# Reordering the start of a fused attention and feed-forward kernel, and moving one transposition from TensorE to DMA

**The chip, the cores and the metric.** The kernel runs on one core of one Trainium2 chip. The metric is the device time of one execution in microseconds; the median of several executions is quoted. The kernel before takes 327.13 us (three runs, 326.89 to 327.17).

Short names used below: TensorE is PE in the profile, its weight loads PEld, VectorE DVE, ScalarE ACT, GpSimd POOL, SyncE SP. A name with a q, such as SPq, is that engine's sequencer, which also issues DMAs.

## The reference

A linear attention (ReLU features weighted by cosine and sine of the position, keys and values summed into one matrix per head) is followed by a feed-forward layer gated with GELU.

```python
# q, k, v: (8 batches, 8 heads, 576 tokens, 64)
q_p, k_p = phi(q), phi(k)                  # relu(x)*cos(pos) next to relu(x)*sin(pos): 128 features
kv  = einsum('bhsf,bhsd->bhfd', k_p, v)
z   = k_p.sum(axis=2)
att = einsum('bhsf,bhfd->bhsd', q_p, kv) / (einsum('bhsf,bhf->bhs', q_p, z)[..., None] + 1e-6)
x   = att laid out as (4608 tokens, 512)
out = (gelu(x @ w_gate) * (x @ w_val)) @ w_out      # 512 -> 1536 -> 512
```

## The kernel before

The attention of one batch has five token tiles, four of 128 tokens and one of 64. The feed-forward layer runs in blocks of tokens: block 0 holds the 576 tokens of batch 0, each later block 512. While block n runs, the attention of batch n + 1 is slipped in between its twelve column tiles. Feed-forward matmuls need the tokens transposed (`xT`). In block 0, and for batch 1, TensorE transposes them into PSUM and another engine copies them out; later batches use a DMA transpose issued by SP.

The parts that matter here (cuts marked):

```python
def x_by_pe(b, t, xb, bank, eng, ..., every=1):      # transposition by TensorE
    ...
    for ct in range(c0, c1):
        nc.tensor.transpose(out=view[:, ct, 0:rows], in_=xb2[...], ...)       # line 343
    cp(xT[...], view[...])                                                    # line 346

def turn_x(b, t, xb):                                # transposition by DMA
    if t < NJ: nc.sync.dma_start_transpose(out=xT[:, :, p0:p0 + 128], in_=xb2)
    else:
        nc.sync.dma_start_transpose(out=xr, in_=xb2)                          # line 208
        nc.gpsimd.tensor_copy(xT[:, :, p0:p0 + 64], xr[:, :, 0:128:2])

# block 0: X(t) = x_by_pe of tile t, Y(t) = its numerators (line 170) and normalization
gate(0, 2, *A, 5); X(2, 0, "v")(); ...
value(0, 2, *A, 7)
gate(0, 3, *A, 4)
Y(3, 0)(); value(0, 3, *A, 2); q_by_pe(0, 4, 3, "s")
gv_unit(0, 0, 256, 128, 5, 6); X(3, 0, "s")()
Y(4, 0)()                                  # writes PSUM banks 0 and 1
gv_unit(0, 1, 256, 128, 4, 7)
...
# before block 1
o_part(0, 3, 5, 0, 5);  x_by_pe(1, 2, y[2], 6, "s")
y4 = numer(1, 4, 0)                        # last 64 tokens of batch 1
o_part(0, 3, 5, 5, 10); x_by_pe(1, 3, y[3], 7, "s")
x_by_pe(1, 4, y4, 6, "v", every=2)
o_part(0, 3, 5, 10, 12)
# block 1: after column tile 0, turn_q(2, ...) issues the DMA transposes of batch 2's queries (line 145);
# after tile 4, kv_half(2, ...) (line 154); within tile 5, the numerators of batch 2's first tile
```

Gate products are line 218, value products 229, output products 259 and, for the last tile, 277.

Of the kernel before, what the change touches and what calls it, by code (L numbers as in the profile page):

```python
# [16 lines left out]
def kernel(  # L17
# [10 lines left out]
    nc = tc.nc  # L28
# [4 lines left out]
    C = H * D  # L33
    J = moe_w_gate.shape[1]
    CT = C // 128
    JT = J // 128
    NJ = 4
# [20 lines left out]
    wo_sb = sb.tile([128, JT, C], BF16, name="wo_sb")  # L58
    xT = sb.tile([128, CT, N_TOK], BF16, name="xT")
    qf = sb.tile([128, H, NJ + 1, D], FP32, name="qf")  # L60
    kf = sb.tile([128, H, NJ + 1, D], FP32, name="kf")
# [68 lines left out]
    def scale(f, j, which, eng, h0=0, h1=H):  # L130
        dst, src = f
        col = (cos_c if which == 0 else sin_c)[:, j:j + 1]
        s, d = src[:, h0:h1, j, :], dst[:, j, h0:h1, which * D:(which + 1) * D]
        if eng == "v":
            nc.vector.tensor_scalar(d, s, col, 0.0, op0=ALU.mult, op1=ALU.max)  # L135
        else:
            nc.scalar.activation(d, s, AF.Relu, scale=col)  # L137
# [30 lines left out]
    def numer_mm(b, t, bank, g, rows=128):  # L168
        for h in range(4 * g, 4 * g + 4):
            nc.tensor.matmul(  # L170
                ps[0:rows, bank + g, (h % 4) * (D + 1):(h % 4 + 1) * (D + 1)],
                lhsT=qT[b % 2][:, t, h, 0:rows],
                rhs=kv[b % 2][:, h, 0:D + 1],
                start=True, stop=True,
            )

    def norm(xb, bank, g0, g1, rows=128):

        n = g1 - g0
        nd = ps[0:rows, bank + g0:bank + g1, 0:4 * (D + 1)].rearrange("p g (h e) -> p g h e", e=D + 1)  # L180
        den = rot.tile([128, 2, 4], FP32, name="den")
        nc.vector.tensor_scalar(den[0:rows, 0:n], nd[:, :, :, D], EPS, None, op0=ALU.add)  # L182
        rec = rot.tile([128, 2, 4], FP32, name="rec")
        nc.vector.reciprocal(rec[0:rows, 0:n], den[0:rows, 0:n])
        nc.vector.tensor_tensor(  # L185
            xb[0:rows, g0:g1], nd[:, :, :, 0:D],
            rec[0:rows, 0:n, :, None].to_broadcast([rows, n, 4, D]), op=ALU.mult,
        )

    def new_xb():  # L190
        return rot.tile([128, 2, 4, D], BF16, name="xb", bufs=4)

    def numer(b, t, bank, rows=128):

        numer_mm(b, t, bank, 0, rows)
        numer_mm(b, t, bank, 1, rows)
        xb = new_xb()
        norm(xb, bank, 0, 2, rows)
        return xb
# [14 lines left out]
    def gate(n, jt, c0, w, gb):  # L214

        p0 = starts[n] + c0
        for ct in range(CT):
            nc.tensor.matmul(  # L218
                ps[:, gb, 0:w], lhsT=wg_sb[:, ct, jt * 128:(jt + 1) * 128],
                rhs=xT[:, ct, p0:p0 + w], start=(ct == 0), stop=(ct == CT - 1),  # L220
            )
        gels[n, jt, c0] = gel = rot.tile([128, 512], FP32, name="gel", bufs=4)
        nc.scalar.activation(gel[:, 0:w], ps[:, gb, 0:w], AF.Gelu)  # L223

    def value(n, jt, c0, w, vb):

        p0 = starts[n] + c0
        for ct in range(CT):
            nc.tensor.matmul(  # L229
                ps[:, vb, 0:w], lhsT=wv_sb[:, ct, jt * 128:(jt + 1) * 128],  # L230
                rhs=xT[:, ct, p0:p0 + w], start=(ct == 0), stop=(ct == CT - 1),
            )
        gel = gels.pop((n, jt, c0))
        nc.vector.tensor_mul(hT[n % 2][:, jt, 64 + c0:64 + c0 + w], gel[:, 0:w], ps[:, vb, 0:w])  # L234

    def gv_unit(n, jt, c0, w, gb, vb, mid=()):
        gate(n, jt, c0, w, gb)
        for f in mid:
            f()
        value(n, jt, c0, w, vb)  # L240
# [15 lines left out]
    def o_part(n, m, bank, j0, j1):  # L256
        c0 = 128 * m - starts[n] + 64
        for jt in range(j0, j1):
            nc.tensor.matmul(  # L259
                ps[:, bank, :], lhsT=hT[n % 2][:, jt, c0:c0 + 128], rhs=wo_sb[:, jt, :],  # L260
                start=(jt == 0), stop=(jt == JT - 1),
            )
        if j1 == JT:
            o_store(m, bank)
# [37 lines left out]
    wo_r = moe_w_out.rearrange("(jt p) c -> p jt c", p=128)  # L302
# [5 lines left out]
    def load_q(b, eng=None):  # L308
        load(qf, q, b, even=eng, odd=eng)

    def load_k(b):
        load(kf, k, b)
# [20 lines left out]
        else:  # L333
            cp(qT[b % 2][:, j, h0:h1, 0:64], qb[:, h0:h1, 0:128:2])

    def x_by_pe(b, t, xb, bank, eng, c0=0, c1=CT, every=1):
        p0 = b * S + t * 128
        cp = nc.vector.tensor_copy if eng == "v" else nc.scalar.copy
        xb2 = xb.rearrange("p g h d -> p (g h d)")
        rows = 128 if t < NJ or every == 2 else 64  # L340
        view = ps[:, bank, 0:256].bitcast(BF16).rearrange("p (c t) -> p c t", c=CT)
        for ct in range(c0, c1):
            nc.tensor.transpose(  # L343
                out=view[:, ct, 0:rows], in_=xb2[0:rows, ct * 128:(ct + 1) * 128], identity=ident[0:rows, 0:rows],
            )
        cp(xT[:, c0:c1, p0:p0 + rows // every], view[:, c0:c1, 0:rows:every])  # L346

    def sq(j, which, eng, *h):
        scale(Q, j, which, eng, *h)
# [37 lines left out]
    numer_mm(0, 1, 0, 1)  # L387
    norm(x1, 0, 0, 2)
    x_by_pe(0, 0, x0, 4, "s", 0, 2)
    dummies(2, 5)  # L390
    x_by_pe(0, 0, x0, 4, "s", 2, 4)
    q_by_pe(0, 2, 3, None)

# [4 lines left out]
    A, Bw = (0, 256), (256, 320)  # L398
    xs = {1: x1}

    def X(t, bank, eng):
        return lambda: x_by_pe(0, t, xs[t], bank, eng)

    def Y(t, bank):
        def f():
            xs[t] = numer(0, t, bank, 128 if t < NJ else 64)
        return f
# [14 lines left out]
    gate(0, 2, *A, 5)  # L422
    X(2, 0, "v")()
    sq(4, 1, "s"), sq(4, 0, "v")
    value(0, 2, *A, 7)
    gate(0, 3, *A, 4)
    Y(3, 0)()
    value(0, 3, *A, 2)
    q_by_pe(0, 4, 3, "s")
    gv_unit(0, 0, 256, 128, 5, 6)  # L430
    X(3, 0, "s")()
    Y(4, 0)()
    gv_unit(0, 1, 256, 128, 4, 7)
    gv_unit(0, 0, 384, 128, 5, 2)
    gv_unit(0, 1, 384, 128, 4, 3)
    gate(0, 4, *A, 5)
# [8 lines left out]


    load_q(1, nc.gpsimd)
    nc.gpsimd.dma_start(out=wo_sb[:, 0:6], in_=wo_r[:, 0:6])
    nc.gpsimd.dma_start(out=wo_sb[:, 6:12], in_=wo_r[:, 6:12])
    nc.gpsimd.tensor_copy(kf[0:2, 0, 0, 0:1], wo_sb[0:2, 5, C - 1:C])  # L450
    load_k(1)
    load(vf, v, 1, 0, 4)
    load(vf, v, 1, 4, 8)
# [1 line left out]
    def L(f, *a):  # L455
        return lambda: f(*a)
# [51 lines left out]
    norm(y[3], 2, 0, 2)  # L508
    o_part(0, 3, 5, 0, 5)
    x_by_pe(1, 2, y[2], 6, "s")  # L510
    y4 = numer(1, 4, 0)
    o_part(0, 3, 5, 5, 10)
    x_by_pe(1, 3, y[3], 7, "s")
    x_by_pe(1, 4, y4, 6, "v", every=2)
    for j in range(NJ + 1):
        sq(j, 0, "v")
    o_part(0, 3, 5, 10, 12)
# [11 lines left out]
    after = {n: {jt: [] for jt in range(JT)} for n in range(NB)}  # L529

    mid = {n: {jt: [] for jt in range(JT)} for n in range(NB)}
    for n in range(1, 7):
        b = n + 1
        a = after[n]

        def put(u, *fs):
            a[u].extend(fs)

        s = 0 if n > 1 else -1
        if n > 1:  # L540
            put(0, L(sq, 0, 0, "v"), L(sq, 1, 0, "v"), L(sq, 1, 1, "v"), L(sq, 0, 1, "s"))
            put(1, L(sq, 2, 0, "v"), L(sq, 2, 1, "s"), L(turn_q, b, 0, 3))
            put(1, L(sq, 3, 0, "v"), L(sq, 4, 0, "v"), L(sq, 4, 1, "v"), L(sq, 3, 1, "s"), L(turn_q, b, 3, 5))
        else:
            put(0, L(sq, 1, 1, "s"), L(sq, 2, 1, "v"), L(turn_q, b, 0, 3))
            put(0, L(sq, 3, 1, "v"), L(sq, 4, 1, "s"), L(turn_q, b, 3, 5))
        put(2 + s, L(sk, 0, 0, "v"), L(sk, 1, 0, "v"), L(sk, 0, 1, "s"), L(sk, 1, 1, "s"))
        put(3 + s, L(sk, 2, 0, "v"), L(sk, 3, 0, "v"), L(sk, 4, 0, "v"))
        put(3 + s, L(sk, 2, 1, "s"), L(sk, 3, 1, "s"), L(sk, 4, 1, "s"), L(cast_v, b, 0, 4))
        put(4 + s, L(cast_v, b, 4, 8, "s"))  # L550
        put(5 + s, L(attn_step, b, 0))
        if b + 1 < B:

            for f, u in zip((load_q, load_k, load_v), (3, 4, 5) if n > 1 else (5, 10, 11)):
                put(u, L(f, b + 1))
        for i in range(5):
            mid[n][6 + s + i].append(L(attn_step, b, i + 1))
# [50 lines left out]
```

## Time and profile before

| | kernel before, the execution first profiled |
|---|---|
| span of the trace | 326.0 us |
| TensorE, VectorE, ScalarE, GpSimd busy | 97, 52, 46, 6% |
| granted TensorE clock | 0.999 |
| TensorE in the chain that ended last | 91% |
| that profiled execution on the clock | 328.16 us |

A trace shows when each instruction ran. "Busy" of TensorE comes from matmul ends that are modelled, so I compare starts: if groups of four 512-column matmuls follow each other every 0.86 us, the engine has no hole there. The execution whose trace I read was 1.03 us slower than the median.

### The profile page before, as it was taken

What the parts mean: (1) busy time and instruction counts of PE and PEld (TensorE: products, weight loads), DVE (VectorE), ACT (ScalarE), POOL (GpSimd) and SP (SyncE); (2) the same over time, 40 slices, a digit from 0 to 9 for tenths busy, and PEclk for the clock granted to TensorE, in tenths of its full rate; (3) what the DMA queues carried; (4) which work ended last, traced back from release to release, by engine and by line L of the source; (5) the groups of instructions that cost most, each with busy time, mean ns of one, the idle gap of its engine ahead of it and who ended that gap; (6) DMA issues with size and microseconds to landing.
All of it is one profiled execution on the core that took longest, in us unless ns stands there. A gap on an engine that the chain in (4) does not pass through costs nothing.

```text
span 326.0 us, 5837 instructions
## 1 busy us (share of the span) xinstructions
PE 315.3 (97%) x2189; PEld 166.8 (51%) x2222; DVE 169.1 (52%) x381; ACT 151.4 (46%) x271; POOL 20.8 (6%) x41
## 2 busy tenths in 40 slices
PE   7789999999999999999999999999999999999994
PEld 3477866455445544554455445544544444444543
DVE  4884676878653667365745374547464222322210
ACT  5674664773474256424652375237622332222321
POOL 2550010000100010001000100000000100100000
PEclk9999999999999999999999999999999999999999
DMA  7999999989999928994799369965533111000024
GB/s 224 285 205 274 193 310 288 343 160 184 284 225 307 274 52 155 298 271 83 149 311 268 81 119 235 356 102 96 131 64 66 42 38 34 32 32 32 35 65 97
DMA packets 87740, 55.43 MB, mean 170 GB/s; under 512 B 52512, under 2 KB 82976, under 8 KB 87712
## 3 DMA queue, kind: packets, MB, share of 16 engines
q1 hardware_dynamic: 81200, 48.71, 60.9%
q0 software_dynamic: 6080, 5.90, 10.1%
q10 hardware_dynamic: 432, 0.46, 0.5%
q8 instruction: 17, 0.28, 0.4%
q14 instruction: 11, 0.09, 0.2%
HBM read 37.75 MB, written 9.44 MB: 145 GB/s over the span
## 4 chain that ended last, share of the span: by engine, by line
PE 91%; DMA 4%; POOL 1%; issue 1%; ACT 0%; SPq 0%; DVE 0%; POOLq 0%; ACTq 0%
PE ps L229 28%; PE ps L218 28%; PE ps L259 28%; PE ps L170 3%; DMA wv_sb<-in_moe_w_val_dram 3%; PE ps L154 3%; DMA qf<-in_q_dram 2%; PE ps L277 1%; PE ps L343 1%; POOL wg_sb L305 0%; PE ps L324 0%; SPq L80 0%; POOL wv_sb L306 0%; ACT xT L346 0%; POOL vf L98 0%
## 5 line engine op out<-in xcount | busy, mean ns | idle before, releaser
L234 DVE TENSOR_TENSOR hT<-gel,ps 128x512 bf16<-128x512 f32 (+5 forms) x126 | 75.9, 607 | 88.7 <-PE ps L229 86.9
L229 PE MATMUL ps<-xT,wv_sb 128*128 128x512 bf16 (+5 forms) x498 | 112.1, 348 | 0.6 <-DMA wv_sb<-in_moe_w_val_dram 0.2
L218 PE MATMUL ps<-xT,wg_sb 128*128 128x512 bf16 (+5 forms) x490 | 111.7, 348 | 0.9 <-issue 0.2
L223 ACT ACTIVATE gel<-ps 128x512 f32<-128x512 f32 (+5 forms) x126 | 67.4, 536 | 75.1 <-PE ps L218 46.5
L259 PE MATMUL ps<-wo_sb,hT 128*128 128x512 bf16 x408 | 94.1, 379 | 0.6
L218 PEld LDWEIGHTS <-wg_sb 128*128 128x128 bf16 x504 | 47.0, 98 | 45.3 <-issue 0.8
L229 PEld LDWEIGHTS <-wv_sb 128*128 128x128 bf16 x504 | 45.6, 98 | 39.6 <-DMA wv_sb<-in_moe_w_val_dram 0.4
L259 PEld LDWEIGHTS <-hT 128*128 128x128 bf16 x420 | 40.7, 98 | 47.8
L288 ACT COPY o_sb<-ps 128x512 f32<-128x512 f32 x35 | 20.5, 586 | 75.4 <-PE ps L259 71.3
L182 DVE TENSOR_SCALAR den<-ps 128x8 f32<-128x8 f32 (+2 forms) x41 | 6.7, 165 | 43.9 <-PE ps L170 43.9
L185 DVE TENSOR_TENSOR xb<-ps,rec 128x512 bf16<-128x512 f32 (+2 forms) x41 | 27.8, 678 | 1.5
L137 ACT ACTIVATE kp<-kf,sin_c 128x512 bf16<-128x512 f32 (+1 forms) x41 | 25.4, 681 | 1.0 <-DMA kf<-in_k_dram 1.0
L170 PEld LDWEIGHTS <-qT 128*128 128x128 bf16 (+1 forms) x320 | 15.1, 98 | 8.7 <-issue 1.0
L135 DVE TENSOR_SCALAR kp<-kf,cos_c 128x512 bf16<-128x512 f32 (+1 forms) x45 | 18.7, 463 | 1.6 <-DMA kf<-in_k_dram 1.6
L137 ACT ACTIVATE qp<-qf,sin_c 128x512 bf16<-128x512 f32 x28 | 19.3, 714 | 0.0
L135 DVE TENSOR_SCALAR qp<-qf,cos_c 128x512 bf16<-128x512 f32 x40 | 18.1, 495 | 0.0
L170 PE MATMUL ps<-kv,qT 128*128 128x65 bf16 (+1 forms) x320 | 16.6, 194 | 0.8 <-ACT xT L346 0.7
L209 POOL COPY xT<-xr 128x256 bf16<-128x256 bf16 x6 | 2.4, 402 | 199.8 <-DMA xr<-xb 199.8
L154 PEld LDWEIGHTS <-kp 128*128 128x128 bf16 x320 | 10.9, 97 | 2.6 <-issue 0.7
L154 PE MATMUL ps<-vx,kp 128*128 128x65 bf16 x320 | 11.1, 193 | 0.1
L127 PE MATMUL ps<-hT 128*128 128x512 bf16 x33 | 9.2, 427 | 1.8 <-DVE par_i L104 1.7
L141 ACT CAST vx<-vf 128x1280 bf16<-128x1280 f32 (+1 forms) x9 | 9.7, 1076 | 1.1 <-DMA vf<-in_v_dram 1.1
(55 smaller groups left out, 89.0 us busy)
## 6 DMA issues: line engine op xcount, KB each, us to landing
out_dram<-o_sb SPq DMA_DIRECT2D x38, 128.0 KB, 2.4
kf<-in_k_dram SPq DMA_DIRECT2D x7, 640.0 KB, 7.8
out_dram<-o_sb SPq DMA_DIRECT2D x16, 256.0 KB, 3.2
qf<-in_q_dram SPq DMA_DIRECT2D x6, 640.0 KB, 6.4
vf<-in_v_dram SPq DMA_DIRECT2D x6, 640.0 KB, 9.6
kf<-in_k_dram SPq DMA_DIRECT2D x7, 512.0 KB, 6.6
qf<-in_q_dram SPq DMA_DIRECT2D x6, 512.0 KB, 4.8
vf<-in_v_dram SPq DMA_DIRECT2D x6, 512.0 KB, 8.6
```

Source lines behind the costliest of these rows:

```text
L135: nc.vector.tensor_scalar(d, s, col, 0.0, op0=ALU.mult, op1=ALU.max)
L137: nc.scalar.activation(d, s, AF.Relu, scale=col)
L141: cp(vx[b % 2][:, :, h0:h1, 0:D], vf[:, h0:h1].rearrange("p h j d -> p j h d"))
L154: nc.tensor.matmul(ps[:, bank, (h % 4) * (D + 1):(h % 4 + 1) * (D + 1)], lhsT=kp[:, j, h, :], rhs=vx[b % 2][:, j, h, 0:D + 1], start=(j == ...
L170: nc.tensor.matmul(ps[0:rows, bank + g, (h % 4) * (D + 1):(h % 4 + 1) * (D + 1)], lhsT=qT[b % 2][:, t, h, 0:rows], rhs=kv[b % 2][:, h, 0:D ...
L185: nc.vector.tensor_tensor(xb[0:rows, g0:g1], nd[:, :, :, 0:D], rec[0:rows, 0:n, :, None].to_broadcast([rows, n, 4, D]), op=ALU.mult,)
L218: nc.tensor.matmul(ps[:, gb, 0:w], lhsT=wg_sb[:, ct, jt * 128:(jt + 1) * 128], rhs=xT[:, ct, p0:p0 + w], start=(ct == 0), stop=(ct == CT - 1),
L223: nc.scalar.activation(gel[:, 0:w], ps[:, gb, 0:w], AF.Gelu)
L229: nc.tensor.matmul(ps[:, vb, 0:w], lhsT=wv_sb[:, ct, jt * 128:(jt + 1) * 128], rhs=xT[:, ct, p0:p0 + w], start=(ct == 0), stop=(ct == CT - 1),
L234: nc.vector.tensor_mul(hT[n % 2][:, jt, 64 + c0:64 + c0 + w], gel[:, 0:w], ps[:, vb, 0:w])
L259: nc.tensor.matmul(ps[:, bank, :], lhsT=hT[n % 2][:, jt, c0:c0 + 128], rhs=wo_sb[:, jt, :], start=(jt == 0), stop=(jt == JT - 1),)
L288: nc.scalar.copy(o_sb, ps[:, bank, :])
```

## The change

It has four parts. (1) At the start, two pieces of ready matmul work are put ahead of two waiting ones. (2) The last 64 tokens of batch 1 are no longer transposed by TensorE before block 1; their numerators move into block 1's first column tile, and the transposition goes to DMA. (3) The output weights are loaded in three pieces, and batch 1's k and v follow the first piece (a fourth of the weights) instead of the first half. (4) Batch 3's queries are loaded earlier in block 1.

```diff
-        rows = 128 if t < NJ or every == 2 else 64        # and the other uses of "every"
+        rows = 128 if t < NJ else 64
     sq(4, 1, "s"), sq(4, 0, "v")
+    gate(0, 3, *A, 4)
     value(0, 2, *A, 7)
-    gate(0, 3, *A, 4)
...
     X(3, 0, "s")()
+    gv_unit(0, 1, 256, 128, 4, 7)
     Y(4, 0)()
-    gv_unit(0, 1, 256, 128, 4, 7)
...
-    nc.gpsimd.dma_start(out=wo_sb[:, 0:6], in_=wo_r[:, 0:6])
-    nc.gpsimd.dma_start(out=wo_sb[:, 6:12], in_=wo_r[:, 6:12])
-    nc.gpsimd.tensor_copy(kf[0:2, 0, 0, 0:1], wo_sb[0:2, 5, C - 1:C])
+    for j0, j1 in ((0, 3), (3, 8), (8, 12)):
+        nc.gpsimd.dma_start(out=wo_sb[:, j0:j1], in_=wo_r[:, j0:j1])
+    nc.gpsimd.tensor_copy(kf[0:2, 0, 0, 0:1], wo_sb[0:2, 2, C - 1:C])
...
-    y4 = numer(1, 4, 0)
     o_part(0, 3, 5, 5, 10)
     x_by_pe(1, 3, y[3], 7, "s")
-    x_by_pe(1, 4, y4, 6, "v", every=2)
...
+    mid[1][0].append(L(attn_step, 1, 5))
...
-            ... (3, 4, 5) if n > 1 else (5, 10, 11)):
+            ... (3, 4, 5) if n > 1 else (1, 10, 11)):
```

More of the change, by code (lines that the diff above doesn't have):

```diff
@@ L334, in q_evac, with x_by_pe @@
             cp(qT[b % 2][:, j, h0:h1, 0:64], qb[:, h0:h1, 0:128:2])
-    def x_by_pe(b, t, xb, bank, eng, c0=0, c1=CT, every=1):
+    def x_by_pe(b, t, xb, bank, eng, c0=0, c1=CT):
         p0 = b * S + t * 128
@@ L345, in x_by_pe @@
             )
-        cp(xT[:, c0:c1, p0:p0 + rows // every], view[:, c0:c1, 0:rows:every])
+        cp(xT[:, c0:c1, p0:p0 + rows], view[:, c0:c1, 0:rows])
     def sq(j, which, eng, *h):
@@ L552 @@
         if b + 1 < B:
-            for f, u in zip((load_q, load_k, load_v), (3, 4, 5) if n > 1 else (5, 10, 11)):
+            for f, u in zip((load_q, load_k, load_v), (3, 4, 5) if n > 1 else (1, 10, 11)):
                 put(u, L(f, b + 1))
```

## The prediction

> **What bounds the kernel now.** I read the page of the profiled execution first, then the waits of each engine, then the chain of waits in two stretches, then the timeline there, and last the DMA queues in short windows.
>
> ```profile
> span 326.0 us, 5837 instructions
> ...
> PE 315.3 (97%) x2189; PEld 166.8 (51%) x2222; DVE 169.1 (52%) x381; ACT 151.4 (46%) x271; POOL 20.8 (6%) x41
> ...
> PE   7789999999999999999999999999999999999994
> ...
> PEclk9999999999999999999999999999999999999999
> ```
>
> TensorE is busy for 97% of the span, every other engine about half or less, and the granted clock never falls. The slices that are not full are the first three (up to about 25 us) and the last. Busy alone would not prove a bound, since matmul ends are modelled; the spacing does. In the chain of waits, steady groups of four 128x512 matmuls take 0.86 us, so 0.216 us each. Any gain must therefore come from less TensorE work, or from holes in TensorE's stream, and after 25 us there are hardly any. These are TensorE's waits in the window 19 to 28 us and, in the fences after, the chain of waits there and around 60 us (columns: start us, us, what):
>
> ```profile
> PE ps L170 <- ACT xT L346: 0.7, 1, 0.7
> ...
> PEld L229 <- DMA wv_sb<-in_moe_w_val_dram: 0.4, 1, 0.4
> PE ps L229 <- DMA wv_sb<-in_moe_w_val_dram: 0.2, 1, 0.2
> ```
>
> ```profile
> 12.40 8.61 DMA wv_sb<-in_moe_w_val_dram
> 21.01 0.05 issue
> ...
> 24.04 0.57 ACT xT L346
> 24.61 0.04 issue
> 24.65 0.42 PE ps L170 x8
> ```
>
> ```profile
> 57.99 0.22 PE ps L343 x4
> 58.21 0.26 PE ps L170 x8
> ...
> 59.54 0.61 PE ps L343 x8
> 60.16 0.43 PE ps L259 x2
> ```
>
> The reader is to see three places. The value product of column tile 2 waits for its weights until 21.01 us. The numerators of batch 0's last tile (line 170, 24.65 us) wait until ScalarE has copied token tile 3 out of the PSUM bank that they write. And at 59.5 us eight transposes take 0.61 us, while four of them elsewhere take 0.22 us.
>
> **What the Trainium skill says.** "TensorE: Matmul & The Clock Gate", section "Wait — 56ns, not 53.3ns?", gives start-to-start times of 55.6 ns for 128 columns and 215.7 ns for 512 once warm. The trace agrees: 0.22 us for four transposes and 0.216 us for one wide matmul. So I count work by spacing, not by the row's mean (348 ns), which overlaps. "PSUM — Partial Sum Buffer", section "PSUM bank collisions raise a hardware error", says two engines must not touch the same bank at the same time and that one should guard by bank; the wait at 24.65 us is such a guard: the transposes of tile 3 use half of bank 0, and the numerators of tile 4 write banks 0 and 1. "DMA: Bandwidth & Descriptors", section "Queues, rings and completion order", says that each DMA engine takes turns between queues, packet by packet. Between 13 and 14 us the GpSimd queue moved 0.15 MB and the SP queue 0.07 MB, so both do run together, though that is a tail and proves no equal shares. The same page, "Issuing engines are not separate DMA queues", says all use the same 16 engines. From 25 to 42 us the trace shows them at 90% or more in every slice, so an earlier load there is bytes moved forward, not bandwidth gained.
>
> **The change, part by part.**
>
> *1. Order at the start.* The timeline of TensorE has: transposes of tile 2 at 20.43 us, so the array is free at 20.43 + 0.22 = 20.65; value of column tile 2 at 21.05. That is a hole of 0.40 us. The gate product of column tile 3 now comes first. It takes 0.44 us (21.50 to 21.94), its weights landed with those of column tile 2, which ran at 20.00, so it just fills the hole: value at 21.09, and the numerators of tile 3 at 21.53 instead of 21.94. From there everything is 0.41 us earlier, if its inputs are. They are not quite. VectorE multiplies column tile 2 at 21.77 to 22.19 as before, then normalizes tile 3: 22.39 to 23.52 before, and directly behind the product now, about 0.2 us earlier, ending at about 23.32. So the transposes of tile 3 start at about 23.37 (before: 23.58), not at 23.17. ScalarE's copy of them took 0.57 us from 24.04 on in the chain; it now runs from about 23.8 to 24.39.
>
> Second hole: transposes at 23.58 + 0.22 = 23.80, numerators of tile 4 at 24.65, so 0.85 us. The gate and value of column tile 1 (25.00 to 25.45, 0.45 us) now go first: 23.59 to 24.04. The numerators wait until about 24.43 and the next work starts 0.35 us later (24.65 to 25.00 before), at 24.78, where it stood at 25.45. **Saved: 0.67 us.** Behind it, tile 4's copy to the activations ended at 27.50 us for a product that started at about 27.54, hence tight; VectorE has one product less between the two, so I expect 0 to 0.1 us to come back. I take 0.65.
>
> *2. The last 64 tokens of batch 1.* Removed from TensorE before block 1: four transposes, with a wait of 0.16 us for the normalized tile (timeline of weight loads at 59.75 us). By the chain, 0.61 - 0.22 = 0.39 us. The eight numerator matmuls stay: about 0.25 us at 58.05 before, about 0.25 us inside block 1 now (steps of 1.98 us in block 1 with such numerators, of 1.73 us without). VectorE loses a copy of 0.42 us. Added: a DMA transpose, a GpSimd copy of 0.40 us, both beside other work. Those of later batches took 2.9 us to land and 0.4 us to copy; started at about 62.6 us this is done by 67 us, and the tokens are read in block 2, at about 96 us. The normalization, about 1.06 us, now sits ahead of block 1's first product on VectorE, which finished 0.1 to 0.2 us late before anyhow; its five scale operations (2.06 us at 60.60) start earlier, since nothing stands in front of them. **Saved: 0.39 us.**
>
> *3. Output weights in three pieces, k and v sooner.* The loads of k wait for the first 6 of 12 row tiles, which ended at 37.9 us. By the windows of the queues, the weights' packets began at about 32.9 us, after the queries, and move 0.2 MB per us; 1.5 MB end at about 40.4. The first 3 tiles are 0.38 MB, so 1.9 us less: k is issued at about 36.1 instead of 38.14. From about 38 us, k's packets compete with 0.45 MB of remaining weights. With half of the turns the weights end at about 42.5 and land at about 44. They are first needed by the ninth output matmul, 46.16 - 0.7 + 8 x 0.216 = 47.2. k and v were not waited for: scaling of k began at 46.15 (ScalarE) and 46.83 (VectorE) straight behind earlier work, and no row of DMA waits stands there. **Saved: nothing**; but it keeps slack that part 1 would have eaten, as the consumers come 0.7 us sooner.
>
> *4. Queries of batch 3 after the second column tile of block 1* instead of the sixth. Issue moves from 74.07 to about 69.8 us, behind the query transposes of batch 2 on the same sequencer (63.81 to 69.78). They are used in block 2, near 97 us. **Nothing.**
>
> Sum: 0.65 + 0.39 = 1.04 us. 327.13 - 1.04 = 326.1.
>
> **The rivals.**
>
> *A: the wait takes the place of the one removed.* If ScalarE's copy of tile 3 came no earlier at all, the numerators would start at 24.65 still and only the 0.45 us of moved work would be won; with part 2, 0.84 us, 326.3. For it: ScalarE runs in order, with a 0.59 us copy and a GELU just ahead of that copy. Against it: both wait for TensorE, which is earlier. A VectorE tail that swallows more would leave about 0.6 us, 326.5.
>
> *B: the output weights arrive late.* If the SP queue, with two sequences of 1.15 MB, took nearly all turns, 0.45 MB of weights would end only after k and v, at about 48.5, land at about 50, and stall TensorE by 2 to 3 us: about 328.5. For it: the SP queue had 86% of the shares against 30% of the other from 10 to 14 us. Against it: there the weights had only just been issued; at 13 to 14 us it was the SP queue that was finishing. I give it 4%.
>
> *C: everything is hidden.* If some later point held the schedule (k, v or the query transposes before block 1), the start's gain would be lost there, and only 0.39 us remains: 326.7. Against it: from 25 us to the end the chain runs on TensorE alone.
>
> *D: all holes close*, 0.40 + 0.85 + 0.39 = 1.64 us: 325.5.
>
> **Range and chances.** The middle is 326.1; A and D bound the mechanism at 325.5 and 326.5. Three runs before spread by 0.28 us, and C is worth 0.6 us more, so 325.4 to 326.9. A 2% change is 6.5 us. All holes of TensorE together are 326.0 - 315.3 = 10.7 us, most of it in stretches that the change does not touch (the first 15 us, the tail), so faster gets 0.01; only something much worse than B reaches slower, 0.01.
>
> **What would show it.** Right: TensorE's matmul count falls by 4; the rows of waits "PE ps L229 <- DMA wv_sb" vanish and the one on ScalarE's copy shrinks to some 0.4 us; in the chain, the first wide output matmul comes 0.6 to 0.7 us sooner (46.16 before), block 1's first gate about 1.0 us sooner (60.44 before); no wait of TensorE on the output weights; one more DMA transpose of that kind (7 instead of 6); the same 0.86 us groups afterwards. Wrong: a wait on the output weights near 47 us; a hole at 26 to 27 us before the column tile that reads token tile 4; a wait of block 1's first value product on VectorE; or output matmuls that start at an unchanged 46.1 us.

## The result

The changed kernel took 327.06 us (four runs, 326.58 to 327.47) against 327.01 for the kernel before (four runs, 326.89 to 327.17). The ratio is 1.0001, with a 95% interval of 0.9983 to 1.0018: the same. A ratio here is the mean time of one kernel's fast runs over the mean of the other's in the same rounds, so it is not quite the ratio of the medians quoted.

The page of the changed kernel:

```profile
span 325.6 us, 5865 instructions
...
PE 318.2 (98%) x2218; PEld 167.1 (51%) x2218; DVE 168.7 (52%) x380; ACT 151.3 (46%) x271; POOL 21.8 (7%) x43
```

Four weight loads are gone (2222 to 2218), as they should be. The matmul count seems to rise from 2189 to 2218, only because the trace of before lacked some matmul records; weight loads are the count to trust. The waits of TensorE over the whole span (the first row, a wait before the first gate that every trace has, is cut, here and below):

```profile
...
PE ps L170 <- DMA qT<-qp: 0.4, 1, 0.4
PE ps L218 <- ACT xT L346: 0.2, 1, 0.2
PE ps L170 <- ACT xT L346: 0.2, 1, 0.2
```

The wait for value weights is gone and the one of the numerators on ScalarE's copy has shrunk from 0.7 to 0.2, as intended. Two rows are new: a gate product waits for ScalarE's copy, and numerators wait for the DMA transpose of the queries. The chain of waits (start, us, what) at the start, around the first gate of block 1, and in block 1:

```profile
23.58 0.60 ACT xT L346
24.18 0.04 issue
24.22 0.41 PE ps L170 x8
```

```profile
58.41 0.24 PE ps L343 x4
58.65 0.02 issue
58.67 0.59 ACT xT L346
59.26 0.04 issue
59.30 1.02 PE ps L218 x4
```

```profile
63.23 7.50 DMA qT<-qp
70.73 0.04 issue
70.78 0.43 PE ps L170 x8
```

In the first, the last numerators still wait, but from 24.22 instead of 24.65. In the second, block 1's first gate (59.30) does not follow the output products before it; it follows ScalarE's copy of token tile 3, which ran from 58.67 to 59.26. In the third, the query transposes of batch 2 were issued at 63.23 us and landed 7.50 us later, and the numerators started only then.

To see where time goes in all runs, I cut the span at starts that the timeline of TensorE shows: first gate product; first output product; block 1's first gate; batch 2's key products; batch 2's first numerators; batch 3's key products; last output tile; end of span. All in us; G is good to about 0.05, since the span is printed to a tenth. The stretch from batch 3's key products to the last output tile is left out: it is 219.62 or 219.63 in every run.

| stretch | before, as read | before again (e1) | changed | changed again (e8) | changed again (e16) |
|---|---|---|---|---|---|
| A: first gate to first output | 29.15 | 28.73 | 28.43 | 28.44 | 28.47 |
| B: to block 1 | 14.28 | 14.29 | 14.03 | 14.03 | 14.04 |
| C: to batch 2's keys | 8.63 | 8.63 | 8.89 | 8.89 | 8.88 |
| D: to its numerators | 2.07 | 2.07 | 2.59 | 2.07 | 2.46 |
| E: to batch 3's keys | 28.35 | 28.38 | 28.03 | 28.03 | 28.05 |
| first gate to last output tile | 302.11 | 301.73 | 301.60 | 301.09 | 301.53 |
| G: last output tile to end | 6.88 | 6.92 | 7.16 | 7.15 | 7.21 |

The time before the first gate is not in it. It ran from 16.16 to 17.50 us over the 19 traces, whatever the kernel; in the latest of them (e4), TensorE waited 1.3 us there for ScalarE's scaled queries. That alone spreads executions by more than what is at stake, and it is why the stretches, which mostly repeat to a few hundredths, tell more than the clock here.

### The profile page after: what moved, and what is told of

It reads as the page before. It is cut to its first block, busy times and chain, and to the rows that moved or that the text cites. A ratio compares the mean times of both kernels' runs of the same rounds, so it can differ in the third digit from the quotient of the medians.

```text
span 325.6 us, 5865 instructions
## 1 busy us (share of the span) xinstructions
PE 318.2 (98%) x2218; PEld 167.1 (51%) x2218; DVE 168.7 (52%) x380; ACT 151.3 (46%) x271; POOL 21.8 (7%) x43
## 4 chain that ended last, share of the span: by engine, by line
PE 94%; DMA 2%; DVE 1%; issue 1%; ACT 1%; ACTq 0%
PE ps L218 28%; PE ps L259 28%; PE ps L229 28%; PE ps L170 3%; PE ps L127 3%; PE ps L154 2%; DMA qT<-qp 2%; PE ps L324 1%; PE ps L277 1%; PE ps L343 1%; DVE vx L141 0%; ACT xT L346 0%; DVE qT L332 0%; DVE qp L135 0%; DVE xb L185 0%
## 5 line engine op out<-in xcount | busy, mean ns | idle before, releaser
L218 PE MATMUL ps<-xT,wg_sb 128*128 128x512 bf16 (+5 forms) x504 | 113.4, 349 | 0.2 <-ACT xT L346 0.2
L259 PE MATMUL ps<-wo_sb,hT 128*128 128x512 bf16 x420 | 96.5, 379 | 0.0
L127 PE MATMUL ps<-hT 128*128 128x512 bf16 x34 | 11.0, 478 | 1.7 <-DVE par_i L104 1.7
```

What stands on the lines that cost most here:

```text
L127: nc.tensor.matmul(ps[:, bank, :], lhsT=junk[:, 0:128], rhs=junk, start=True, stop=True)
L218: nc.tensor.matmul(ps[:, gb, 0:w], lhsT=wg_sb[:, ct, jt * 128:(jt + 1) * 128], rhs=xT[:, ct, p0:p0 + w], start=(ct == 0), stop=(ct == CT - 1),
L259: nc.tensor.matmul(ps[:, bank, :], lhsT=hT[n % 2][:, jt, c0:c0 + 128], rhs=wo_sb[:, jt, :], start=(jt == 0), stop=(jt == JT - 1),)
```

## The experiments

All used the kernel before in the same rounds. The first four ran on one chip, the next four on another, then four, three and two on further jobs; kernels are compared by the clock only within such a group.

### e1: the kernel before, again

No edit.

> The kernel before, unchanged, as a control. The execution that the prediction was read from took 328.16 us on the clock, its three timed sisters 326.89 to 327.17, so its trace may hold some 1.0 us that the kernel does not usually lose. Theory Q (a queue: the added DMA transpose of the last 64 tokens stands ahead of batch 2's query transposes and delays them; the base is sound): ratio 1.000, span 325.9 to 326.1, and the trace again has TensorE's wait of 0.4 us for the value weights (21.05 us). Theory B (the base was a bad draw: part of the holes that I read were chance): ratio 1.000, span 325.0 to 325.3, and the wait for the value weights is gone or under 0.15 us.

Measured: 327.34 us median (327.10 to 327.62), ratio 1.0000 (0.9988 to 1.0012), span 325.4. Its waits of TensorE, over the whole span:

```profile
...
PE ps L170 <- ACT xT L346: 0.7, 1, 0.7
PE ps L218 <- DMA xT<-xb: 0.2, 1, 0.2
```

There is no wait for value weights. Stretch A is 28.73 instead of 29.15 us: the wait for the value weights, the hole of 0.40 us that I had counted first, is not in every execution. Of four traces with the old order at the start, two have it (before 29.15, e3 29.12) and two do not (e1 28.73, e5 28.74). Theory B is right in that the hole is not always there, though the span fell only to 325.4; and e3 has it in an execution of 327.27 us, below its group's median for the kernel before, so it does not mark a slow execution. The second row is another hole, near 83 us, of 0.3 us by spacing: it is 0.31 and 0.34 in the two traces of the kernel before, and part of stretch E. It stands before block 2's first gate. That gate reads tokens up to the fourth tile of batch 2 (tile 3, counted from 0), which come by the DMA transposes of line 205. The SP queue of the trace first read shows what stood ahead of them, the loads of batch 3's queries:

```profile
74.07 1.36 SPq L80 DMA_DIRECT2D qf<-in_q_dram  x2
75.54 4.34 SPq L205 DMA_TRANSPOSE xT<-xb  x3
```

The last of those three landed at 83.71 and the gate started at 83.95; in e1 it was 83.07 and 83.32. What this means for part 4 of the change is told under "The sum".

### e2: only the order at the start

```diff
+    gate(0, 3, *A, 4)
     value(0, 2, *A, 7)
-    gate(0, 3, *A, 4)
...
+    gv_unit(0, 1, 256, 128, 4, 7)
     Y(4, 0)()
-    gv_unit(0, 1, 256, 128, 4, 7)
```

> Only the new order at the start (gate of column tile 3 ahead of value of tile 2; gate and value of tile 1 ahead of the last numerators). My step 1 and theory Q: the prefix gains 0.65 us, nothing later gives it back (batch 2's query transposes keep about 1 us of slack), ratio 0.9980, about 326.35 us. Theory B: only the second hole is typical, so 0.25 to 0.45 us are gained, ratio 0.9986 to 0.9992. If both fail (no gain): ratio 1.000, and some later wait of TensorE must be longer by 0.65 us.

Measured: 326.97 us (326.88 to 327.78), ratio 0.9995 (0.9982 to 1.0007). Stretch A is 28.53; B, C and D are those of the kernel before. The gain against e1 is 0.20 us, below even theory B's range, and with the changed kernel's 28.43 it is 0.30. Against the two old-order traces with the wait for the weights it would be 0.6 to 0.7. So 0.65 is what the order saves in some executions, not in all.

### e3: only the last 64 tokens by DMA

```diff
-    y4 = numer(1, 4, 0)
-    x_by_pe(1, 4, y4, 6, "v", every=2)
+    mid[1][0].append(L(attn_step, 1, 5))
```

> Only the last 64 tokens of batch 1 moved to a DMA transpose in block 1. My step 2 without a queue effect: 0.39 us gained, ratio 0.9988. Theory Q: TensorE reaches block 1 about 0.3 us sooner, the query transposes of batch 2 land 1 to 2 us later than before (before: issued 63.81, landed 69.4), and the numerators of batch 2's first tile (71.14 before) wait 0 to 0.5 us for them; net ratio 0.9990 to 1.0005. Also expected: block 1's first gate waits about 0.2 us for ScalarE's copy of the third tile, which the transposes used to hide.

Measured: 327.64 us (326.86 to 328.39, six runs), ratio 1.0009 (0.9994 to 1.0023). B is 14.03 and C 8.88. So B fell by 0.26 where 0.64 was due (0.39 of transposes and 0.25 of numerators that went to C), and C rose by 0.25: together nothing was gained. The trace has the wait of the gate product on ScalarE's copy. D is 2.17, that is, 0.10 of waiting: the query transposes were issued at 63.32, landed 7.1 us later at 70.42, and were needed at 70.35.

### e4: the changed kernel, with the DMA turn later

```diff
-    mid[1][0].append(L(attn_step, 1, 5))
+    mid[1][2].append(L(attn_step, 1, 5))
```

> The changed kernel, with the numerators and the DMA transpose of the last 64 tokens in column tile 2 of block 1 instead of tile 0, thus behind batch 2's query transposes on the queue. Theory Q: the query transposes land about 69.3 us, TensorE does not wait for them, the changed kernel's 0.4 to 0.5 us at 70.78 us are won back: about 0.5 us below the changed kernel, ratio to before 0.9980 to 0.9986. Theory B alone, or a wait whose cause is the earlier load of batch 3's queries: the wait of TensorE on the query transposes stays at 0.4 us, ratio as the changed kernel, 1.000.

Measured: 327.61 us (327.20 to 328.44), ratio 1.0010 (0.9997 to 1.0024). The waits of TensorE, whole span:

```profile
...
PE ps L324 <- ACT qp L137: 1.3, 1, 1.3
PE ps L218 <- ACT xT L346: 0.2, 1, 0.2
PE ps L170 <- ACT xT L346: 0.2, 1, 0.2
```

The row on the query transposes is gone and D is 2.06, as theory Q said: they landed at 69.40, 1.57 us before they were needed. But the clock did not fall. This execution started late (1.3 us in the first row), and its end was odd: G is 7.96 us. That had not been expected.

### e5: only the weight pieces and the loads of k and v

```diff
-    (two pieces of six; k and v behind the first)
+    for j0, j1 in ((0, 3), (3, 8), (8, 12)): ...
+    nc.gpsimd.tensor_copy(kf[0:2, 0, 0, 0:1], wo_sb[0:2, 2, C - 1:C])
```

> Only the output weights in three pieces and the loads of k and v behind the first of them. My step 3: no change of time; in the trace the k loads are issued at about 36.1 us instead of 37 to 38, TensorE has no wait on the output weights, the stretch from the first gate to the first output matmul is 28.7 us and from there to block 1 14.29 us, as in the control. A rival that the rest of the weights arrives late would show a wait at about 47 us and 0.5 to 3 us more.

Measured: 327.30 us (327.00 to 327.38), ratio 1.0001 (0.9988 to 1.0013). The SP queue's timeline:

```profile
35.03 1.32 SPq L80 DMA_DIRECT2D kf<-in_k_dram  x2
```

The loads came sooner (38.14 us in the trace first read), and nothing came of it, as predicted: A 28.74, B 14.28, C 8.63, D 2.08, and TensorE waits on no output weights. E is 28.03: the hole near 83 us is absent here.

### e6: the changed kernel without the DMA turn

```diff
+    y4 = numer(1, 4, 0)
     o_part(0, 3, 5, 5, 10)
     x_by_pe(1, 3, y[3], 7, "s")
+    x_by_pe(1, 4, y4, 6, "v", every=2)
-    mid[1][0].append(L(attn_step, 1, 5))
```

> The changed kernel without the DMA turn: order, loads and the earlier queries of batch 3 only, the last 64 tokens by TensorE as before. Theory Q plus the swap of waits seen in the traces: first gate to first output matmul 28.43 (as changed), output matmul to block 1 14.28 (as before), block 1 to batch 2's key products 8.63, those to the first numerators 2.07 (no wait on the query transposes, against 2.59 in the changed kernel). So about 0.5 us better than the changed kernel over these stretches and about 0.3 better than the control; on the clock 0.9985 to 0.9995, near what the clock can tell. If instead the earlier load of batch 3's queries delays the transposes, the stretch stays near 2.5.

Measured: 326.78 us (326.60 to 327.06), ratio 0.9988 (0.9975 to 1.0000). A 28.44, B 14.29, C 8.63, D 2.06, E 28.04, G 6.93. Part 4 stays in this kernel and D shows no wait, so the earlier load of batch 3's queries is not what delays the transposes. B + C is 22.92, exactly that of the changed kernel (14.03 + 8.89): giving four transposes back to TensorE costs nothing.

### e7: later turn, and the transposes of tile 3 earlier

```diff
-    o_part(0, 3, 5, 5, 10)
+    o_part(0, 3, 5, 5, 8)
     x_by_pe(1, 3, y[3], 7, "s")
...
-    o_part(0, 3, 5, 10, 12)
+    o_part(0, 3, 5, 8, 12)
-    mid[1][0].append(L(attn_step, 1, 5))
+    mid[1][2].append(L(attn_step, 1, 5))
```

> The changed kernel with the DMA turn in column tile 2 (behind the query transposes) and with the transposes of token tile 3 two output matmuls (0.43 us) sooner, so that ScalarE's copy of them is done before block 1's first gate. If the swap theory holds (the 0.39 us of removed transposes came back as a wait of 0.40 us for that copy), the stretch from the first output matmul to block 1 falls from 14.03 to 13.63 to 13.68 us and TensorE's wait on the copy vanishes; together with the queue fix about 1.0 us less than the control between the first gate and the last output tile (about 300.7 against 301.73), ratio 0.9965 to 0.9980. If the wait has another cause, 14.03 stays.

Measured: 326.74 us (326.60 to 327.15), ratio 0.9991 (0.9977 to 1.0005). B is 13.62: the copy's wait is gone, and the 0.41 us is there. That shows the swap: e4 and e7 differ only in where those transposes stand. First gate to last output tile is 300.81, 0.92 under e1. But G is 7.71, 0.79 above e1, and takes nearly all of it.

### e8: the changed kernel, again

No edit to the changed kernel.

> The changed kernel once more, on the chip and in the rounds of the others. Theory Q: its stretches repeat: 28.43, 14.03, 8.89 us, and 2.4 to 2.6 for the last (key products of batch 2 to first numerators, with a wait on the query transposes); first gate to last output tile 301.5 to 301.6; start and end differ by up to 1 us from run to run. Ratio 0.999 to 1.001.

Measured: 326.77 us (326.56 to 327.42), ratio 0.9991 (0.9977 to 1.0005). A, B, C and G repeat, but D is 2.07: no wait. The transposes were issued at 62.86 and landed at 69.66, 0.23 us before they were needed. My expectation of 2.4 to 2.6 was wrong; the wait comes in some executions only.

### e10: the DMA turn issued twice

```diff
             nc.sync.dma_start_transpose(out=xr, in_=xb2)
+            if b == 1: nc.sync.dma_start_transpose(out=rot.tile([128, CT, 128], BF16, name="xr"), in_=xb2)
```

> The changed kernel with the suspected cost doubled: the DMA transpose of the last 64 tokens is issued twice (the second copy is not used), ahead of batch 2's query transposes. So far the stretch from batch 2's key products to its first numerators was 2.07 us without any such transpose ahead (five kernels), 2.17 with one (alone), 2.59 and 2.07 with one in two executions of the changed kernel. Theory Q (each transpose ahead delays the query transposes by one to two us, and the slack is about used up): the stretch grows to 3 to 4.5 us and TensorE waits on the query transposes for 1 to 2.5 us. If 2.59 was an accident with another cause: 2.07 to 2.6.

Measured: 327.04 us (two runs), ratio 0.9996 (0.9976 to 1.0015), D 2.55. In the waits of TensorE:

```profile
PE ps L170 <- DMA qT<-qp: 0.3, 1, 0.3
```

A miss in size. The query transposes landed at 70.41, which is within what one turn gives. Doubling did not double the delay. What this leaves of theory Q is in the table of all landings below: a transpose ahead costs the slack, but the cost is not so much per transpose. The trace tells why in part: the two turns landed at 67.38 and 67.73, only 0.35 us apart, so most of the second one's time lay beside the first one's.

### e9, e11 and e12: fewer pieces, another bank

e9 is e7 with the output weights in two pieces. e11 is e7 with

```diff
-    X(3, 0, "s")()
-    gv_unit(0, 1, 256, 128, 4, 7)
-    Y(4, 0)()
+    X(3, 7, "s")()
+    gv_unit(0, 1, 256, 128, 4, 3, (Y(4, 0),))
```

so that the last numerators of batch 0 no longer share a PSUM bank with the transposes ahead of them. e12 is e11 with two pieces.

> The version with the later DMA turn and the earlier transposes of tile 3, but with the output weights in two pieces as before. Same TensorE stretches as with three pieces: 28.43 to 28.53, 13.62, 8.95, 2.06 us, first gate to last output tile 300.7 to 300.85, thus 0.9 us under the control. The open point is the end: last output tile to the end of the span was 6.88 to 6.93 us in six kernels, 7.15 in the changed one, 7.7 to 8.0 in the two versions with the later turn. If the number of GpSimd loads matters to the end, it goes back to 6.9 here and the ratio is 0.9970; if the place of the turn matters, 7.7 stays and the ratio is 0.9985 to 0.9990.

> The version with the later turn and the earlier transposes of tile 3, and batch 0's tile 3 transposed into PSUM bank 7 instead of 0, so that the numerators of tile 4 (banks 0 and 1) need not wait for its copy; they run between gate and value of column tile 1. If the bank is what they wait for, TensorE's wait on ScalarE's copy (about 0.4 us by spacing) vanishes and the first stretch is 28.05 to 28.2 us instead of 28.43. If VectorE's normalization is the next thing to wait for, a wait on it takes the place and 28.4 stays. Ratio 0.9960 to 0.9985, depending on the end of the program (7.7 or 6.9 us after the last output tile).

> The same with the output weights in two pieces. First stretch 28.05 to 28.2 us, first gate to last output tile about 300.4 us, 1.3 us under the control. With an end of 6.9 us the ratio is 0.9955 to 0.9965, with 7.7 us about 0.998.

Measured: e9 327.41 us, 1.0003 (0.9991 to 1.0016); e11 327.17, 1.0000 (0.9988 to 1.0013); e12 327.45, 1.0005 (0.9991 to 1.0019). e9 has G 7.66, so two pieces do not cure that end. In e11, TensorE's waits from 19 to 28 us are one row:

```profile
PE ps L229 <- DVE hT L234: 0.5, 1, 0.5
```

The wait on the copy vanished, so the bank was what the numerators waited for. But a value product now waits for VectorE to read bank 3, which my edit used twice in a row, and A became 28.79 (e11 and e12) instead of 28.43. A wait took the place of a wait, this time by my own doing. G was 7.65 and 7.33.

### e13, e14 and e15: turn at tile 0 or 1, transposes of tile 3 earlier

e13 is the changed kernel with e7's two `o_part` edits alone; e14 is e13 with two weight pieces; e15 is e13 with the turn in `mid[1][1]`.

> The changed kernel with only the transposes of token tile 3 moved two output matmuls up. The copy's wait vanishes (output matmul to block 1 13.62 us, as seen with the later turn); the turn stays ahead of the query transposes and TensorE now comes 0.4 us sooner, so the wait on them should show in the trace at 0.2 to 0.9 us (stretch 2.3 to 3.0). If the place of the turn decides the end, it is 7.15 us as in the changed kernel. First gate to last output tile 300.9 to 301.6, ratio 0.9975 to 1.0000.

> The same with the output weights in two pieces. In the run with the turn alone and two pieces the end was 6.88 us, in the changed kernel with three 7.15: if the pieces together with the turn make the 0.27 us, the end is 6.9 here and 7.15 in the run beside it; if not, both are equal. Stretches as in the run beside it. Ratio 0.997 to 0.9995.

> Transposes of tile 3 up, three pieces, and the turn in column tile 1: it is queued right behind the query transposes and ahead of batch 3's queries. Theory Q: no wait on the query transposes, stretch 2.06 to 2.08, landing 1 us or more before it is needed; first gate to last output tile 300.8. If the later place of the turn makes the end longer whatever the exact place: 7.7 us and an instruction packet in the last 6 us; if only the place behind batch 3's queries does: 7.15 and no such packet. Ratio 0.9970 to 0.9990.

| | median us | ratio (95%) | B | D | first gate to last output tile | G |
|---|---|---|---|---|---|---|
| e13 | 326.62 | 0.9977 (0.9964 to 0.9989) | 13.63 | 2.49 | 301.12 | 7.22 |
| e14 | 326.81 | 0.9980 (0.9967 to 0.9994) | 13.63 | 2.30 | 300.93 | 6.82 |
| e15 | 326.91 | 0.9983 (0.9970 to 0.9995) | 13.63 | 2.07 | 300.69 | 7.94 |

The chain of waits of e13 around block 1's first gate, and later at the numerators:

```profile
57.31 0.22 PE ps L343 x4
57.53 0.86 PE ps L259 x4
58.40 0.86 PE ps L218 x4
...
62.16 7.40 DMA qT<-qp
69.56 0.05 issue
69.61 0.43 PE ps L170 x8
```

Four output products stand between transposes and gate, and the gate follows them at once; ScalarE's copy is hidden. Being sooner, TensorE then waits for the query transposes. All three are faster than the kernel before by a little (0.2%, far under 2%), and their intervals leave out 1; but they share one set of runs of the kernel before, so they are not three independent proofs. The waits of the SP queue in the last 6 us, in e13's two neighbours, tell about the end. First e14, then e15:

```profile
SPq L602 <- DMA out_dram<-o_sb: 1.5, 3, 0.9
...
SPq L602 <- PEq L602: 0.7, 2, 0.5
```

```profile
SPq L602 <- DMA out_dram<-o_sb: 2.1, 2, 1.7
SPq L602 <- PEq L602: 1.0, 2, 0.8
```

and the DMA queues of e15 in the same window:

```profile
q14 instruction: 1, 0.01, 0.7%
```

Line 602 is the end of the program. Over all traces: with the turn ahead of the query transposes and three pieces, the step put down to PEq is 0.8 to 0.9 (changed kernel three times 7.15 to 7.21, e10 7.18, e13 7.22, and the repeat e17 7.16); with two pieces, 0.5 (e3 6.88, e14 6.82); without the turn 0.5 (6.88 to 6.93). With the turn behind the query transposes (e4, e7, e9, e11, e12, e15), an instruction packet of queue 14 falls in the last 6 us, where no other kernel looked at there has one, and G is 7.33 to 7.96. So the end depends on both the place of the turn and the pieces. That the late instruction packet causes it is likely but only argued: I have no run that moves the packet alone.

### e16 and e17: the changed kernel and e13 side by side

> The changed kernel, third profile. Stretches 28.43, 14.03, 8.89 us, then 2.07 to 2.6 for the one with the wait on the query transposes, an end of 7.15 us. Ratio to before 0.999 to 1.000.

> The version with the transposes of tile 3 two output matmuls up, second profile, beside the changed kernel. Stretches 28.43, 13.63, 8.89, then 2.2 to 2.6, an end of 7.2 us. Between 0 and 0.4 us under the changed kernel, since the copy's 0.40 us are gone and the wait on the query transposes can take up to all of it; ratio to before 0.9975 to 0.9990. Clearly apart from the changed kernel only if the queue wait takes little.

Measured: e16 326.70 us (326.44 to 327.52), 0.9989 (0.9976 to 1.0002), D 2.46. e17 326.65 us (326.36 to 327.16), 0.9988 (0.9976 to 1.0000), B 13.62, D 2.07 (2.2 to 2.6 was expected: another miss), first gate to last output tile 300.68. The two are not apart on the clock. e13's edit beats the kernel before in one group; that it beats the changed kernel is not shown.

### All landings of batch 2's query transposes

Landing is the issue plus its time to landing; slack is the start that D = 2.07 would give less the landing, to about 0.05 us.

| turn | slack, us (wait, us) |
|---|---|
| by TensorE, or none: before, e1, e2, e5, e6 | 1.73, 0.94, 1.23, 1.74, 1.43 (none waits) |
| DMA, behind the query transposes: e4, e7, e9, e11, e12, e15 | 1.57, 1.18, 1.20, 1.55, 1.15, 1.16 (none waits) |
| DMA, ahead: e3, changed, e8, e16 | -0.07, -0.47, 0.23, -0.35 (0.10, 0.52, 0, 0.39) |
| DMA, ahead: e13, e14, e17 | -0.37, -0.19, 0.56 (0.42, 0.23, 0) |
| DMA, ahead, twice: e10 | -0.48 (0.48) |

All eleven traces without a turn ahead have D of 2.06 to 2.08. Of the seven with one turn ahead, five wait and two do not (e8, e17). This is what shows the turn's place on the queue as the cause. The loss has two parts. With the turn ahead, whose issue takes SP 1.2 us, the query transposes are issued 7.0 us before they are needed, against 7.3 us without it and 7.7 to 7.8 us with it behind them (5.7 us with two turns ahead). And in all seven traces they land 2.5 to 2.7 us after the turn (in e10, 2.7 us after the second one), however late that is.

## Why the prediction was wrong

It said 326.1 us, range 325.4 to 326.9, and it was 327.06. That the change would stay within 2% was right; the expected gain of 1.04 us was not there.

**Step 1, "I take 0.65".** Against the execution I had read, the step is right: A went from 29.15 to 28.43, 0.72 us, and the mechanism of each hole was as described. But the term of the first hole was mis-sized: it was read off one execution and taken to be always there. The wait for the value weights is in two of the four traces with the old order; without it the order saves 0.30 (28.73 to 28.43), and the mean of A over those four is 28.94, so about 0.5 us is saved on average. There was a warning to look twice, 328.16 us for that execution against 327.13 for the median, though this hole explains only 0.4 of it.

**Step 2, "Saved: 0.39 us".** This step failed. Removing the transposes took 0.39 us of work out, and block 1's first gate then waited 0.40 us for ScalarE's copy of tile 3, which those transposes had been hiding. B + C is 22.92 both with them (e1, e6) and without (changed, e8). Two things misled me. I had looked at what the moved work waits for, not at what waits behind it: the copy takes 0.59 us and only 0.43 us of output products were left after its transposes. And the row of waits says 0.2 where spacing says 0.40, since the ends of matmuls are modelled: two output matmuls from 58.47 to 59.30 is 0.83 us, against 0.43 for two elsewhere. The Trainium skill says the same ("Perfetto Trace Analysis", section "Tensor Engine Instruction (MATMUL, LD_WEIGHTS)": the end is estimated from the instruction's size).

The sentence that the DMA transpose runs "beside other work" was the second fault of this step. It is not on TensorE, but it is on a queue, in front of something TensorE needs. I had noted that the loads of batch 3's queries are issued behind the query transposes and did not ask the same of the turn. It was issued at 61.85 and took 6.4 us instead of the 2.9 that I had assumed, with the queue still busy with earlier transfers (0.78 MB from 61 to 63 us); the query transposes then landed 7.50 us after issue instead of 5.6 to 6.4. This cost 0, 0.39 and 0.52 us in three executions. The Trainium skill has the ground for it ("DMA: Bandwidth & Descriptors", section "Queues, rings and completion order": each engine consumes a ring's descriptors in order), and the traces agree: the query transposes land 2.5 to 2.7 us after the turn in all seven. The cost is not additive (e10).

**Step 3, "nothing".** Right (e5); k was issued at 36.13 us in the changed kernel, where I had worked out 36.1.

**Step 4, "nothing".** The reading was wrong. Block 2 does not begin near 96 us but at 83.95, and batch 3's queries are first scaled at 85.51; the last 64 tokens, too, are read from 83.95 on. These loads also stood ahead of the transposes that block 2's first gate waits for (see e1), so moving them had something to win.

**The sum.** Put against e1 and averaged over the three traces of the changed kernel: A -0.28, B + C 0, D +0.30, E -0.34, G +0.25. The sum is -0.07 us, which is the unchanged time within noise; with the mean of the four old-order traces in place of e1's A it would be about -0.3. The clock's three comparisons (1.0001, 0.9991, 0.9989) cannot tell these apart. E is the hole near 83 us, of which the trace I read had a row ("issue", 0.2 us) that I passed over. Part 4 stands in 14 traces: the last transpose that the gate needs landed 0.3 to 2.0 us before the gate, and none has the hole. It is missing from five: three have the hole (before, e1 and, half as long, e2), with the gate 0.25 us behind the landing, and two (e3, e5) escape it with a landing 0.1 to 0.3 us ahead. So part 4 most likely won E; no run changes part 4 alone. (E is 0.13 us longer in e9 and e12 for another reason, at numerators near 78 us, which was not looked into.) I foresaw neither E nor G.

**The rivals.** The mechanism of A, a wait in the place of the one removed, was right but sat in step 2, where I had not looked, not in step 1. B, late output weights, did not happen. C came nearest: a later point, the query transposes, took back part of the start's gain, only it was batch 2's in block 1 and was itself made by the change. Of the signs that I listed for "wrong", none was the one that showed. The gate of block 1 came 1.14 us sooner in the changed trace, which I had named as a sign of being right; 0.17 of that was a luckier start, 0.72 the first hole's bad draw and the order, and 0.25 merely numerators put off until after it. A milestone just before the moved work is paid for proves little.

## What to carry to other kernels

Before taking work off the bounding engine, ask what finishes behind that work: a copy hidden by it can become a wait of about the same size (here 0.40 us for 0.39). Here the removal showed in the stretches only once the copy's producer stood two matmuls earlier: B fell from 14.03 to 13.63 (e13), and the wait in the queue took up to 0.42 us of that back. A DMA that is "beside other work" still stands in a queue, so look at what is issued behind it and how much slack that has. When the stake is under 1 us, profile the kernel before twice: compare the profiled execution's own time with the median, and compare stretches between landmarks, not whole spans.

## What the Trainium skill lacked or had wrong

- "DMA: Bandwidth & Descriptors", section "DMA Transpose (X-bar)", has no time for a transpose queued behind other transfers. Here the turns of later batches landed 2.4 to 3.7 us after issue and batch 1's, behind other transfers, 5.3 to 6.7 us (3.0 in e15). One turn ahead of the query transposes took their slack from 0.94 to 1.74 us down to -0.47 to 0.56 us; a second turn ahead added little (slack -0.48).
- The same page's "Latency and other measured facts" gives 261 GB/s for a DMA transpose with a non-contiguous middle dimension, but nothing on what a queued transpose waits before its data move. In the changed kernel the DMA engines moved 290 GB/s from 68 to 70 us, with the query transposes in the queue; from 64 to 68 us, with the turn in it too, they moved 75 GB/s on average, with long stretches in which next to nothing moved. A time worked out from the rate alone would miss these stretches.
- No page says that the end of a program changes when instructions are moved elsewhere in it. From the last output tile to the end of the span it was 6.82 to 6.93 us, 7.15 to 7.22 us or 7.33 to 7.96 us, by the place of one DMA transpose and by whether a weight load has two pieces or three.
